# GpSimd subtracts one weight chunk of a tile instead of three in the first expert mixture

## The chip, the core and the metric

The kernel runs on one core of a Trainium2 chip. The metric is device time in microseconds (us) of one execution. The engines are named as the profile names them: PE is TensorE (matrix products), PEld its weight loads, DVE is VectorE, ACT is ScalarE, POOL is GpSimd, SP is SyncE, which issues most transfers.

## What is computed

An attention over 4 batches, 8 heads and 576 positions, whose weights far below the row's maximum are dropped, makes 2304 tokens of 512 numbers. They go through two mixtures of eight experts. An expert is two matrix products with a rectifier between them. The first mixture sends a token to its best expert; the second deals the tokens out so that each expert gets 288.

```python
# first mixture (cut)
e_idx = np.argmax(x @ w_gate, axis=1)
for e in range(E):                      # E = 8, D = 512, F = 1024
    mask = e_idx == e
    h = np.maximum(x[mask] @ w1[e], 0.0)
    ye = h @ w2[e]
    out[mask] = gate_w[mask, None] * eom[mask, e, None] * ye
```

## The kernel before

The first mixture, `moe1`, works on tiles of 128 tokens of one expert: 23 tiles (0 to 22), and two more that are only run if the routing needs them. `run` goes over the tiles, one turn of its loop for each. The order on each engine is that in which the code is written.

The weights of an expert come as eight chunks of 128x1024: chunks 0 to 3 are rows of `w1`, chunks 4 to 7 rows of `w2`. For a product of nearly float32 accuracy each chunk is split: `wh` is the chunk rounded (a cast on ScalarE, L609), `wl` is the chunk minus `wh` (L610 on GpSimd, L611 on VectorE). TensorE then makes three products for each pair of operands, high by high, high by low and low by high. Activations are split in the same way: `xh` and `xl` from the transposed tokens (L621), `hh` and `hl` from the transposed hidden layer (L649, L650). A chunk is split again for each tile that uses it.

`split(t,c)` splits chunk c for tile t and issues SyncE's conditional load of that chunk for the next expert. `splits(n)` calls it along a list: chunks 0 to 3 of tile t+2 come after chunks 4 to 7 of tile t. There are seven buffers each for `wh` and `wl`, so a cast waits until TensorE is done with the chunk seven places earlier.

A turn t does this, in the order of the code: `splits` issues chunks 4, 5 and 6 of tile t; `mm1` makes the first half of tile t+1's first product (L633 to L635); `ey` evicts the finished output y of tile t-1 from PSUM on VectorE (L667); `hT` transposes the hidden layer of tile t (Th, L647) and splits it into hh and hl; `splits` issues chunk 7 of tile t and chunk 0 of tile t+2; `mm1` makes the rest of tile t+1's first product; `yT` transposes y (Ty, L673); GpSimd gathers the tokens of tile t+3 (L615); `xT` transposes those of tile t+2 (Tx, L619) and splits them; in odd turns `logits2` transposes two tiles' router sums (Tl, L684); `splits` issues chunks 1, 2 and 3 of tile t+2; `mm2` makes tile t's second product (L660 to L662); in even turns `logits` makes the router sums. Th, Ty, Tx, Tl and those sums share three PSUM buffers (`psT`), handed out in turn, so a transpose waits until the reader of the one three places back is done. In turn 21 VectorE also finds a maximum between y and hl (`reach`, with a copy fmb of one row, L696).

Who subtracts is decided in `split`: GpSimd takes chunk 2 from tile 3 on, chunk 5 from tile 1 on and chunk 7 from tile 2 on; VectorE takes the rest.

Of the kernel before, what the change touches and what calls it, by code (L numbers as in the profile page):

```python
# [9 lines left out]
F32 = mybir.dt.float32  # L10
# [549 lines left out]
def moe1(tc, K, r, rts, xd, w1, w2, wg2, ys, LG2, reach_, ahead):  # L560
# [3 lines left out]
    nc=tc.nc; ident=K['ident']; N=NT1  # L564
    with ExitStack() as ctx:
# [7 lines left out]
        def rv(c,par): return raw[c][:,ds(par,1),:].rearrange("p a f -> p (a f)")  # L573
# [25 lines left out]
        def prefetch(t,c):  # L599
            q=regs[t]; nc.sync.dma_start(rvd(c,q['o']),src(q['n'],c),cond=q['c'],cond_hint=(t%3==0))  # L600
# [6 lines left out]
        def split(t,c):  # L607
            q=regs[t]; h,l=wtile()
            nc.scalar.copy(h,rv(c,q['a']))  # L609
            if t>(2 if c==2 else 0 if c==5 else 1 if c==7 else N): nc.gpsimd.tensor_sub(l,rv(c,q['p']),h.bitcast(F32))  # L610
            else: nc.vector.tensor_sub(l,rv(c,q['v']),h.bitcast(F32))  # L611
            prefetch(t,c); W[t,c]=(h,l)
        def gather(t):
# [97 lines left out]
        def splits(ahead):  # L711

            nonlocal pos
            while pos<min(used+ahead,ends[cur[0]]):
                t,c=order[pos]; pos+=1
                if c==0: regload(t)
                if t==0 and c<6: prefetch(t,c)
                else: split(t,c)
# [412 lines left out]
```

## Time and profile before

| what | value |
|---|---|
| median of 3 runs (lowest to highest) | 946.09 us (945.7 to 946.3) |
| profiled execution, its own time | 945.42 us |
| span of the profile | 943.6 us |
| busy over the span: PE, DVE, ACT, POOL | 94%, 77%, 67%, 41% |
| mean granted TensorE clock | 0.981 of full speed |
| first mixture, first and last VectorE subtraction | 341.3 to 644.3 us |

The busy shares are means over stages with different limits: attention, the first mixture, the routing of the second, the second mixture. The change touches the first mixture alone, so its stretch is what to read. A row of a timeline gives the start and the duration; rows of one kind that follow without a gap are merged, with their count (x3) and their whole duration; in brackets stands the idle time before, and what ended it.

### The profile page before, as it was taken

Reading aid. Unit: us, or ns where it says so; the run is one execution under the profiler, and the core shown is the slowest. Engines: PE = TensorE matmul, PEld = TensorE weight load, DVE = VectorE, ACT = ScalarE, POOL = GpSimd, SP = SyncE. Lnnn points to the kernel's source line nnn. Section 1 sums busy time; section 2 is a strip of 40 time slices with the busy share of each in tenths; the row PEclk is TensorE's granted clock in tenths of the full one; section 3 lists DMA queues with packets and bytes.
Section 4 is the critical chain, followed back from the end, with each engine's and each line's share of the span. In section 5 each row is a group of like instructions: output and inputs, shape, how many; then the busy total and the mean of one; then the engine's idle time right before and its main releaser. Section 6 shows DMA issues by size and latency. Waiting matters only on the chain. (4 is left out here: it accounts for less than half of the span.)

```text
span 943.6 us, 18044 instructions
## 1 busy us (share of the span) xinstructions
PE 886.3 (94%) x5939; PEld 733.2 (78%) x5939; DVE 725.2 (77%) x1191; ACT 635.6 (67%) x1070; POOL 384.7 (41%) x391
## 2 busy tenths in 40 slices
PE   7899999999999999899999999998779999999995
PEld 6677777777777667678787777786449999999994
DVE  5898988888888789798999998987755555555540
ACT  5787878878977677677787788774315555555541
POOL 4234323433431324577777776774030221122211
PEclk9999999999999999999999999999779999999998
DMA  7534444544331670155544655111535666666500
GB/s 190 149 88 124 122 118 115 130 128 115 104 83 53 221 259 25 44 163 185 170 154 148 211 168 182 43 36 46 180 117 180 194 192 186 179 193 203 162 26 25
DMA packets 69346, 127.64 MB, mean 135 GB/s; under 512 B 14912, under 2 KB 27200, under 8 KB 69248
## 3 DMA queue, kind: packets, MB, share of 16 engines
q1 hardware_dynamic: 64016, 109.91, 38.4%
q0 software_dynamic: 5232, 16.52, 5.6%
q8 instruction: 49, 0.80, 0.4%
q14 instruction: 49, 0.40, 0.1%
HBM read 159.70 MB, written 15.99 MB: 186 GB/s over the span
## 5 line engine op out<-in xcount | busy, mean ns | idle before, releaser
L611 DVE TENSOR_TENSOR wl<-raw,wh 128x1024 fp32r<-128x1024 f32 x115 | 218.1, 1916 | 28.4 <-ACT wh L609 28.1
L610 POOL TENSOR_TENSOR wl<-raw,wh 128x1024 fp32r<-128x1024 f32 x63 | 167.6, 2662 | 102.2 <-ACT wh L609 101.4
L609 ACT CAST wh<-raw 128x1024 fp32r x178 | 177.7, 1064 | 4.0 <-PE Y L662 3.3
L469 ACT ACTIVATE e<-S,nm 128x576 f32<-128x576 f32 x144 | 107.8, 749 | 55.0 <-DVE nm L464 54.6
L464 DVE TENSOR_REDUCE nm<-S 128x1 f32<-128x576 f32 x144 | 108.4, 757 | 21.8 <-PE S L388 10.6
L499 DVE SCALAR_TENSOR_TENSOR a<-S,th,e 128x576 f32<-128x576 f32 x144 | 114.4, 814 | 11.1 <-ACT e L469 4.8
L966 DVE TENSOR_TENSOR wl<-raw,wh 128x1024 fp32r<-128x1024 f32 x60 | 73.4, 1225 | 36.9 <-ACT wh L966 36.9
L1037 POOL DMA_INDIRECT out_dram<-o,it x24 | 22.4, 934 | 173.0 <-ACT o L1031 154.1
L397 PE MATMUL T<-ident,a 128*128 128x128 f32 x576 | 86.6, 273 | 0.0
L1008 PE MATMUL H<-xh,wh 128*128 128x288 f32 x256 | 77.8, 304 | 0.1
L1020 PE MATMUL Y<-hh,wh 128*128 128x288 f32 x256 | 77.5, 303 | 0.0
L318 POOL TENSOR_TENSOR ql<-f,QH 64x512 fp32r<-64x512 f32 x30 | 38.2, 1274 | 94.5 <-ACT f L317 76.4
L419 PE MATMUL O<-aT,v 128*64 128x288 f32 x512 | 75.8, 418 | 0.5 <-ACT xt L424 0.5
L1009 PE MATMUL H<-xl,wh 128*128 128x288 f32 x256 | 75.6, 295 | 0.2 <-DVE xl L1002 0.2
L633 PE MATMUL H<-wh,xh 128*128 128x512 f32 x184 | 75.1, 408 | 0.7 <-ACT xh L621 0.7
L1021 PE MATMUL Y<-hl,wh 128*128 128x288 f32 x256 | 75.5, 295 | 0.0
L1022 PE MATMUL Y<-hh,wl 128*128 128x288 f32 x256 | 75.5, 295 | 0.0
L402 ACT COPY aT<-T 128x512 f32<-128x512 f32 x128 | 75.2, 588 | 0.2 <-PE T L397 0.2
L660 PE MATMUL Y<-wh,hh 128*128 128x512 f32 x184 | 74.5, 405 | 0.9 <-ACT wh L609 0.9
L1010 PE MATMUL H<-xh,wl 128*128 128x288 f32 x256 | 75.3, 294 | 0.0
L662 PE MATMUL Y<-wh,hl 128*128 128x512 f32 x184 | 72.3, 393 | 0.0
L661 PE MATMUL Y<-wl,hh 128*128 128x512 f32 x184 | 72.3, 393 | 0.0
(344 smaller groups left out, 2130.4 us busy)
## 6 DMA issues: line engine op xcount, KB each, us to landing
raw<-in_moe_w_dram SPq DMA_DIRECT2D x256, 512.0 KB
ys<-y SPq DMA_DIRECT2D x23, 256.0 KB
q<-in_q_dram SPq DMA_DIRECT2D x16, 256.0 KB
k<-in_k_dram SPq DMA_DIRECT2D x16, 256.0 KB
v<-in_v_dram SPq DMA_DIRECT2D x16, 256.0 KB
QA<-QH SPq DMA_DIRECT2D x32, 128.0 KB
QB<-QH SPq DMA_DIRECT2D x32, 128.0 KB
xd<-xr SPq DMA_DIRECT2D x16, 256.0 KB
```

The lines of the kernel that those rows point to most:

```text
L397: for kb in (2*part,2*part+1): nc.tensor.transpose(TT[n][:,kb,:],a[:,o+kb*P:o+(kb+1)*P],ident)
L419: nc.tensor.matmul(O[hd*64:hd*64+64,:288],L['v'][:,hd,kb,:],aT[hd][:,kb,cs],start=kb==0,stop=False,skip_group_check=True)
L464: nc.vector.tensor_reduce(nm[:,i:i+1],S[i][:,:,:288],axis=AX.XY,op=ALU.max,negate=True)
L469: nc.scalar.activation(e[i],S[i][:,:,:288],AF.Exp,bias=nm[:,i:i+1])
L499: nc.vector.scalar_tensor_tensor(a[:,hd*576:hd*576+576].rearrange("p (a b) -> p a b",a=2),S[i][:,:,:288],th[:,i:i+1],e[i],op0=ALU.is_ge,op ...
L609: nc.scalar.copy(h,rv(c,q['a']))
L610: if t>(2 if c==2 else 0 if c==5 else 1 if c==7 else N): nc.gpsimd.tensor_sub(l,rv(c,q['p']),h.bitcast(F32))
L611: else: nc.vector.tensor_sub(l,rv(c,q['v']),h.bitcast(F32))
L1008: nc.tensor.matmul(H[:,:288],wh[:,fs],xh[:,kc],start=kc==0,stop=False)
L1009: nc.tensor.matmul(H[:,:288],wh[:,fs],xl[:,kc],start=False,stop=False)
L1020: nc.tensor.matmul(Y[:,:288],wh[:,ds_],h,start=f==0,stop=False)
L1021: nc.tensor.matmul(Y[:,:288],wh[:,ds_],l,start=False,stop=False)
```

## The change

One condition in `split`: which engine subtracts which chunk. GpSimd now takes chunk 6 from tile 2 on, and chunk 5 of tile 1. All the rest goes to VectorE. Casts, loads, products and buffers stay as they are.

```diff
             nc.scalar.copy(h,rv(c,q['a']))
-            if t>(2 if c==2 else 0 if c==5 else 1 if c==7 else N): nc.gpsimd.tensor_sub(l,rv(c,q['p']),h.bitcast(F32))
+            if t>0 and c==(5 if t==1 else 6): nc.gpsimd.tensor_sub(l,rv(c,q['p']),h.bitcast(F32))
             else: nc.vector.tensor_sub(l,rv(c,q['v']),h.bitcast(F32))
```

In the built program's order the chunks are told apart by their buffers: raw_4548 is chunk 0, raw_4549 chunk 1, and so on to raw_4555, chunk 7. A row ISA sets a register for the row after it, TENSOR_LOAD reads one.

VectorE at the start of turn 2, from chunk 0 of tile 3 to the eviction y of tile 1. Before:

```order
L611 TENSOR_TENSOR wl<-raw_4548,wh 128x1024
L611 ISA
L611 TENSOR_TENSOR wl<-raw_4549,wh 128x1024
L611 ISA
L611 TENSOR_TENSOR wl<-raw_4551,wh 128x1024
L611 ISA
L611 TENSOR_TENSOR wl<-raw_4552,wh 128x1024
L611 ISA
L611 TENSOR_TENSOR wl<-raw_4554,wh 128x1024
L667 TENSOR_SCALAR y<-Y,gs 128x512
```

And in the changed kernel, the same place on VectorE:

```order
L611 TENSOR_TENSOR wl<-raw_4548,wh 128x1024
L611 ISA
L611 TENSOR_TENSOR wl<-raw_4549,wh 128x1024
L611 ISA
L611 TENSOR_TENSOR wl<-raw_4550,wh 128x1024
L611 ISA
L611 TENSOR_TENSOR wl<-raw_4551,wh 128x1024
L611 ISA
L611 TENSOR_TENSOR wl<-raw_4552,wh 128x1024
L611 ISA
L611 TENSOR_TENSOR wl<-raw_4553,wh 128x1024
L667 TENSOR_SCALAR y<-Y,gs 128x512
```

Chunks 2 and 5 have come in ahead of y, and chunk 6 has left: six subtractions stand there instead of five, and the last one before y is that of chunk 5.

VectorE in an odd turn, from the last subtraction ahead of y to the first one behind xl (LG is the reading of the transposes Tl). Before:

```order
L611 TENSOR_TENSOR wl<-raw_4554,wh 128x1024
L667 TENSOR_SCALAR y<-Y,gs 128x512
L650 TENSOR_TENSOR hl<-Th,hh 128x512 x2
L605 TENSOR_LOAD tab
L605 ISA x2
L611 ISA
L611 TENSOR_TENSOR wl<-raw_4548,wh 128x1024
L621 TENSOR_TENSOR xl<-Tx,xh 128x512
L685 TENSOR_REDUCE LG_71<-Tl 128x16
L611 ISA
L611 TENSOR_TENSOR wl<-raw_4549,wh 128x1024
```

And in the changed kernel, the same stretch on VectorE:

```order
L611 TENSOR_TENSOR wl<-raw_4553,wh 128x1024
L667 TENSOR_SCALAR y<-Y,gs 128x512
L650 TENSOR_TENSOR hl<-Th,hh 128x512 x2
L611 ISA
L611 TENSOR_TENSOR wl<-raw_4555,wh 128x1024
L605 TENSOR_LOAD tab
L605 ISA x2
L611 ISA
L611 TENSOR_TENSOR wl<-raw_4548,wh 128x1024
L621 TENSOR_TENSOR xl<-Tx,xh 128x512
L685 TENSOR_REDUCE LG_71<-Tl 128x16
```

Chunk 7 has come in between hl and chunk 0 of the tile after next.

GpSimd, from one tile's last subtraction to the next tile's, in any turn from 3 on. Before:

```order
L610 TENSOR_TENSOR wl<-raw_4555,wh 128x1024
L605 TENSOR_LOAD tab
L605 ISA x2
L615 DMA x<-xd,ix_4728 128x512
L610 ISA
L610 TENSOR_TENSOR wl<-raw_4550,wh 128x1024
L610 ISA
L610 TENSOR_TENSOR wl<-raw_4553,wh 128x1024
L610 ISA
```

And in the changed kernel, on GpSimd:

```order
L610 TENSOR_TENSOR wl<-raw_4554,wh 128x1024
L605 TENSOR_LOAD tab
L605 ISA x2
L615 DMA x<-xd,ix_4728 128x512
L610 ISA
L610 TENSOR_TENSOR wl<-raw_4554,wh 128x1024
```

One subtraction and one gather are left in a turn, and the gather stands behind chunk 6 instead of chunk 7.

## Rows read from the trace of the kernel before

**Rows 1.** The page's costliest groups: the subtractions of both mixtures.

```profile
L611 DVE TENSOR_TENSOR wl<-raw,wh 128x1024 fp32r<-128x1024 f32 x115 | 218.1, 1916 | 28.4 <-ACT wh L609 28.1
L610 POOL TENSOR_TENSOR wl<-raw,wh 128x1024 fp32r<-128x1024 f32 x63 | 167.6, 2662 | 102.2 <-ACT wh L609 101.4
...
L966 DVE TENSOR_TENSOR wl<-raw,wh 128x1024 fp32r<-128x1024 f32 x60 | 73.4, 1225 | 36.9 <-ACT wh L966 36.9
```

**Rows 2.** Busy time by stretch: us, PE, PEld, DVE, ACT, POOL, PEclk, DMA.

```profile
380.00:385.00 5.00, 4.47 (x17) 3.66 (x18) 4.47 (x6) 3.60 (x5) 1.33 (x2) 0.66 0.38 108
480.00:520.00 40.00, 39.71 (x205) 32.32 (x204) 37.26 (x30) 32.32 (x43) 29.40 (x13) 1.00 0.43 146
```

**Rows 3.** TensorE's waits, 330 to 660 us: total us, times, longest.

```profile
PE Ty L673 <- DVE y L667: 5.4, 10, 3.5
```

**Rows 4.** Timeline of TensorE in an even turn: start, us, operation.

```profile
489.75 0.39 PE L634 MATMUL H<-wl,xh 128*128 128x512 f32 x1
489.98 0.40 PE L635 MATMUL H<-wh,xl 128*128 128x512 f32 x1
...
490.95 0.47 PE L660 MATMUL Y<-wh,hh 128*128 128x512 f32 x1
```

**Rows 5.** Timeline of TensorE in the odd turn after it.

```profile
503.42 0.39 PE L635 MATMUL H<-wh,xl 128*128 128x512 f32 x1
504.04 0.63 PE L673 MATMUL Ty<-ident,y 128*128 128x128 f32 x4 [0.23 <-DVE y L667]
...
505.14 0.44 PE L684 MATMUL Tl<-ident,ls 128*128 128x128 f32 x2
505.34 0.48 PE L660 MATMUL Y<-wh,hh 128*128 128x512 f32 x1
```

**Rows 6.** Timeline of TensorE in turn 2.

```profile
376.69 0.39 PE L635 MATMUL H<-wh,xl 128*128 128x512 f32 x1
380.53 0.63 PE L673 MATMUL Ty<-ident,y 128*128 128x128 f32 x4 [3.46 <-DVE y L667]
...
384.89 0.39 PE L662 MATMUL Y<-wh,hl 128*128 128x512 f32 x1
```

**Rows 7.** Timeline of TensorE in turn 21.

```profile
638.46 0.39 PE L635 MATMUL H<-wh,xl 128*128 128x512 f32 x1
...
642.00 0.48 PE L660 MATMUL Y<-wh,hh 128*128 128x512 f32 x1
```

**Rows 8.** Timeline of VectorE in the odd turn of rows 5.

```profile
498.67 1.23 DVE L611 TENSOR_TENSOR wl<-raw,wh 128x1024 fp32r<-128x1024 f32 x1 [0.66 <-ACT wh L609]
500.56 2.67 DVE L611 TENSOR_TENSOR wl<-raw,wh 128x1024 fp32r<-128x1024 f32 x1 [0.67 <-ACT wh L609]
503.15 0.74 DVE L667 TENSOR_SCALAR y<-Y,gs 128x512 f32<-128x512 f32 x1
503.81 1.27 DVE L650 TENSOR_TENSOR hl<-Th,hh 128x512 fp32r<-128x512 f32 x2
```

**Rows 9.** Timeline of GpSimd in the same turn.

```profile
499.66 2.49 POOL L610 TENSOR_TENSOR wl<-raw,wh 128x1024 fp32r<-128x1024 f32 x1 [2.73 <-ACT wh L609]
502.78 2.69 POOL L610 TENSOR_TENSOR wl<-raw,wh 128x1024 fp32r<-128x1024 f32 x1 [0.63 <-ACT wh L609]
```

**Rows 10.** Timeline of ScalarE in the same turn.

```profile
497.58 2.94 ACT L609 CAST wh<-raw 128x1024 fp32r x3
500.68 1.07 ACT L649 CAST hh<-Th 128x512 fp32r<-128x512 f32 x2
```

**Rows 11.** Timeline of VectorE ahead of y in turn 2.

```profile
367.40 12.32 DVE L611 TENSOR_TENSOR wl<-raw,wh 128x1024 fp32r<-128x1024 f32 x5
```

**Rows 12.** Timeline of ScalarE at the same place.

```profile
370.82 2.94 ACT L609 CAST wh<-raw 128x1024 fp32r x3
```

**Rows 13.** Timeline of VectorE in turn 21.

```profile
639.13 1.42 DVE L696 COPY fmb<-fm 1x128 f32<-1x128 f32 x1
```

**Rows 14.** Timeline of GpSimd in turn 21.

```profile
637.81 2.67 POOL L610 TENSOR_TENSOR wl<-raw,wh 128x1024 fp32r<-128x1024 f32 x1 [0.64 <-ACT wh L609]
```

## The prediction

> **What bounds the kernel now.** I read the page's costliest groups first. The change touches two lines of the same subtraction: VectorE does it 115 times at a mean of 1916 ns, GpSimd 63 times at 2662 ns, and the second mixture's copy of it, where GpSimd subtracts nothing, takes VectorE only 1225 ns for the same shape [rows 1]. So something in the first mixture makes VectorE's subtraction 0.69 us longer, 115 times.
>
> Then the busy time by stretch. In 40 us from the middle of the first mixture TensorE is busy for 39.71, VectorE for 37.26, ScalarE for 32.32, GpSimd for 29.40 [rows 2]. TensorE bounds the stage, so the change can give back only the time in which TensorE stands still and waits for VectorE. Those waits are few: ten times the transposes of a finished output tile (Ty, L673) wait for its eviction y (L667), 5.4 us in all, of which one wait is 3.5 [rows 3].
>
> A wait as the list shows it is less than what the turn loses, so I measure in TensorE's own order, from the start of the last matmul of L635 in a turn to the first one of L660. In an even turn, in which nothing waits, this is 489.98 to 490.95, 0.97 us; neighbouring matmuls start 0.23 us apart [rows 4]. An odd turn has two more transposes (Tl, 505.14 to 505.34, 0.20 us), so undisturbed it would take 1.17; it takes 503.42 to 505.34, 1.92 [rows 5]. So an odd turn loses 0.75 us: to y, then to the PSUM buffers that hl frees for Tx and Tl. Turns are 13.44 us apart (489.98 to 503.42).
>
> The long wait is in turn 2: 3.46 us for y. Behind it the transposes and nine matmuls, 376.69 to the start of 384.89, take 8.20 us [rows 6]. Undisturbed it would be 0.97 and then 8 steps of 0.23: 2.8. So this place loses 5.4 us, 3.46 of it the wait itself and most of the rest the clock: from 380 to 385 the granted clock is 0.66 of full speed [rows 2], a mixture of the 1.2 and 2.4 GHz levels after the engine had stood still.
>
> The third place is turn 21: from 638.46 to 642.00, 3.54 us against 1.17, a loss of 2.37 [rows 7].
>
> **Why VectorE is late there.** Lay VectorE's and GpSimd's rows of an odd turn side by side. The subtraction at 498.67 meets no GpSimd work and takes 1.23 us. The next, at 500.56, takes 2.67 and ends at 503.23 [rows 8]; GpSimd's subtraction runs from 499.66 to 502.15 [rows 9]. VectorE ends 1.08 us after GpSimd ends: it did nothing until then. In the other direction, GpSimd's next one starts at 502.78, while VectorE's subtraction runs to 503.23, and takes 2.69, ending 2.24 after that. The two subtractions exclude each other. But y (0.74) and both hl (1.27 for two) run at 503.15 and 503.81, inside that GpSimd row, at full speed: they read PSUM. So three GpSimd subtractions a tile hold up VectorE in SBUF work, except for what falls on y and hl.
>
> **The change, part by part.** From turn 3 on GpSimd loses chunks 2, 5 and 7 and gets 6: 63 subtractions become 22 (21 of chunk 6, and chunk 5 of tile 1 as before), and VectorE's 115 become 156.
>
> VectorE's load. Seven subtractions of 1.23, y 0.74, two hl 1.27 and xl, about as long as one hl (0.64): 11.3 us in a turn of 13.44. Now it is 37.26/40 of 13.44, 12.5. The two added subtractions cost 2.5 and the blocked time that goes is larger.
>
> Odd turns (3, 5, ... 19, nine of them). ScalarE's casts of chunks 4, 5, 6 run from 497.58 to 500.52, about 0.98 apart, and hh is done at 501.75 [rows 10]; these stay. VectorE: chunk 4 498.67 to 499.90, chunk 5 to 501.1, y to 501.85, both hl to 503.1. TensorE can ask for y at 503.65 (0.23 after its last L635), for the buffers of Tx and Tl at about 504.0 and 504.35. All come earlier by 1.2 us or more, so the 0.75 goes whole. GpSimd's chunk 6 has its cast at 500.52, must wait for VectorE's chunk 5 until 501.1, and takes 2.4: 503.5. Chunk 6 is read 12 matmuls into the second product, 504.6 + 12 x 0.23 = 507.4: hidden, and without cover up to 3.9 us of delay would cost nothing. Chunk 7, now behind hl on VectorE, waits for that port until 503.5 and ends at 504.7; it is read at 504.6 + 18 x 0.23 = 508.7. xl and the next chunk 0 stand behind it; ScalarE's part of xl comes after 505, as now. The even turns lose nothing now and have the same margins. Nine times 0.75 is 6.75 us.
>
> Turn 2. VectorE has five subtractions from 367.40 on that take 12.32 us, to 379.7, and then y [rows 11]. It will have six (chunks 0 to 3 of tile 3, then 4 and 5 of tile 2), with no GpSimd work beside them. Four end at 367.40 + 4 x 1.22 = 372.3; the casts of 4, 5, 6 end by 373.76 [rows 12], so 4 and 5 end at 374.7, y at 375.5, hl at 376.7. TensorE wants y at 376.92. The wait goes and with it the slow clock: 5.4 us. From both sides: nothing if another wait ends last there, 5.4 at most.
>
> Turn 21. A copy fmb of one row, between y and hl, takes 1.42 us and ends at 640.55 [rows 13], 0.07 after GpSimd's chunk 7 ends (637.81 + 2.67 = 640.48) [rows 14]. That subtraction moves to VectorE, behind hl. Chunk 6 is left ahead of fmb; placed as in an odd turn, where it ends 0.15 before Ty is wanted, it ends at about 638.5, so fmb at 638.6 and hl at 639.9, against 639.4 at which Tl wants it. Some 0.5 us stays: 2.37 - 0.5 = 1.9. The bounds are 1.0 (fmb held its whole 1.4 again) and 2.37.
>
> Other queues. GpSimd's gather stood behind chunk 7 and stands behind chunk 6: earlier. SyncE's conditional loads wait for each subtraction in order; those of 2, 5 and 7 are released sooner, that of 6 at 503.5 instead of 503.23. The stages behind the first mixture start from its last tile and move with it.
>
> Sum: 6.75 + 5.4 + 1.9 = 14.05 us. The profiled execution took 945.42 us (span 943.6), so 931.4; the median of the runs shown is 0.67 higher, 946.09, so **932.0 us**, 1.5% less.
>
> **A rule against it.** The row of 500.56 shows a float32 subtraction that takes 1.4 us longer than the one at 498.67 and ends 1.08 us after GpSimd's [rows 8, 9]. The Trainium skill, Advanced Engine Details and Errata, VectorE Performance Modes, ties the blocking of GpSimd and VectorE to VectorE's two-port modes, for which it names conditions; no row says whether this subtraction is in one. [...]
>
> **Rivals.** (1) The odd turns hand their wait on: ScalarE, 32.32 of 40 busy, or a PSUM buffer ends last instead of VectorE. For it: ScalarE's work does not shrink. Against: hh was done at 501.75, 1.9 us before Ty. Then only turns 2 and 21 pay: 945.42 - 7.3 + 0.67 = 938.8. Chance 0.12.
> (2) Turn 2 keeps its wait, because a cast or gather was about to end as late: 945.42 - 8.65 + 0.67 = 937.4. Chance 0.07.
> (3) Slower: VectorE is not given back what GpSimd took. Its subtractions stay at the present length for another reason, and two more of 1.23 make 12.5 + 2.46 = 15.0 us of work in a turn of 13.44, 1.5 over in each of 20 turns: 946.09 + 31 = 977. It decides from a net addition of 0.92 us a turn, the present idle time. The rows of 1225 ns and 1.23 speak against it. Chance 0.04.
> (4) No change that can be told: the waits move elsewhere in all three places. 946, chance 0.03.
> My forecast has the remaining 0.74.
>
> **How the numbers follow.** A measurement of this kernel can tell about 0.2%, 1.9 us. The forecast alone, with the bounds of turn 21 and a few tenths in the nine odd turns, is 930 to 934. The range must also take in rivals 1 and 2: 929.5 to 939. Faster 0.93 (forecast and rivals 1, 2), same 0.03, slower 0.04.
>
> **What would show it.** VectorE's subtraction in the mixture should fall from 1916 ns to under 1400, its busy share there below 90%; the ten waits of Ty for y should be gone, the clock between turns 2 and 3 full, and the three distances 0.97, 1.17 and about 1.7 us. It is wrong if Tx or Ty wait for a ScalarE line, if L661 or L634 wait for wl, or if VectorE's subtractions keep 1.9 us.

## The result and the profile after

The changed kernel takes 931.34 us (median of 4 runs, 930.74 to 931.51), the kernel before 946.19 beside it: a ratio of 0.9841, 95% interval 0.9825 to 0.9856. The forecast was 932.0, with 929.5 to 939.0 as its range. The profiled execution took 930.74 us, its span is 928.6 against 943.6.

The page's groups of the subtractions, after (answering to [rows 1]):

```profile
L611 DVE TENSOR_TENSOR wl<-raw,wh 128x1024 fp32r<-128x1024 f32 x156 | 187.9, 1256 | 23.7 <-ACT wh L609 21.2
...
L610 POOL TENSOR_TENSOR wl<-raw,wh 128x1024 fp32r<-128x1024 f32 x22 | 63.4, 2882 | 197.4 <-ACT wh L609 91.1
```

VectorE makes 41 subtractions more and is busy with them for 30 us less: their mean fell from 1916 to 1256 ns, next to the 1225 of the second mixture. The busy time by stretch (us, PE, PEld, DVE, ACT, POOL, PEclk, DMA; answering to [rows 2]):

```profile
370.00:380.00 10.00, 10.00 (x54) 8.40 (x53) 9.72 (x11) 9.92 (x15) 4.49 (x2) 1.00 0.17 54
380.00:385.00 5.00, 5.00 (x28) 3.58 (x27) 3.28 (x4) 3.01 (x5) 0.00 (x0) 1.00 0.01 2
480.00:520.00 40.00, 40.00 (x214) 32.43 (x213) 32.91 (x35) 33.21 (x45) 11.32 (x6) 1.00 0.43 141
```

In the middle of the mixture TensorE is busy for 40.00 of 40 us instead of 39.71, VectorE for 32.91 instead of 37.26, GpSimd for 11.32 instead of 29.40. Where the clock had fallen to 0.66 after turn 2 it is now 1.00 throughout.

TensorE's waits from 330 to 660 us (total, times, longest; answering to [rows 3]); the ten waits of Ty for y are gone, and a new one stands there, for A:

```profile
PE cn L836 <- DVE G L832: 4.4, 2, 3.2
PE Ty L673 <- DVE A L698: 1.1, 1, 1.1
```

(The row of cn belongs to the routing of the second mixture, which has moved into this window.) The timeline of TensorE: an even turn, an odd turn, turn 2 and turn 21, from the last matmul of L635 to the first of L660 (answering to [rows 4 to 7]):

```profile
480.35 0.40 PE L635 MATMUL H<-wh,xl 128*128 128x512 f32 x1
...
481.31 0.46 PE L660 MATMUL Y<-wh,hh 128*128 128x512 f32 x1
...
493.77 0.40 PE L635 MATMUL H<-wh,xl 128*128 128x512 f32 x1
494.00 0.60 PE L673 MATMUL Ty<-ident,y 128*128 128x128 f32 x4
494.36 0.54 PE L619 MATMUL Tx<-identr,x 128*128 128x128 f32 x4
494.74 0.41 PE L684 MATMUL Tl<-ident,ls 128*128 128x128 f32 x2
494.90 0.48 PE L660 MATMUL Y<-wh,hh 128*128 128x512 f32 x1
...
375.46 0.39 PE L635 MATMUL H<-wh,xl 128*128 128x512 f32 x1
375.69 0.60 PE L673 MATMUL Ty<-ident,y 128*128 128x128 f32 x4
...
376.42 0.46 PE L660 MATMUL Y<-wh,hh 128*128 128x512 f32 x1
...
624.89 0.40 PE L635 MATMUL H<-wh,xl 128*128 128x512 f32 x1
...
626.27 0.48 PE L660 MATMUL Y<-wh,hh 128*128 128x512 f32 x1
```

The distances are 0.96, 1.13, 0.96 and 1.38 us, where they were 0.97, 1.92, 4.75 and 3.54. Nothing in brackets stands at Ty: it no longer waits for y. (The 4.75 of turn 2 is 376.69 to 381.44; the prediction's 8.20 takes in eight matmuls more.) The timeline of VectorE in the odd turn and ahead of y in turn 2, and behind it that of GpSimd in the odd turn (answering to [rows 8, 9, 11]):

```profile
489.02 2.36 DVE L611 TENSOR_TENSOR wl<-raw,wh 128x1024 fp32r<-128x1024 f32 x2 [1.71 <-ACT wh L609]
491.29 0.74 DVE L667 TENSOR_SCALAR y<-Y,gs 128x512 f32<-128x512 f32 x1
491.95 1.28 DVE L650 TENSOR_TENSOR hl<-Th,hh 128x512 fp32r<-128x512 f32 x2
493.15 2.71 DVE L611 TENSOR_TENSOR wl<-raw,wh 128x1024 fp32r<-128x1024 f32 x2
...
366.57 6.89 DVE L611 TENSOR_TENSOR wl<-raw,wh 128x1024 fp32r<-128x1024 f32 x6
373.38 0.74 DVE L667 TENSOR_SCALAR y<-Y,gs 128x512 f32<-128x512 f32 x1
```

```profile
491.02 2.63 POOL L610 TENSOR_TENSOR wl<-raw,wh 128x1024 fp32r<-128x1024 f32 x1 [10.87 <-PE Th L647]
```

GpSimd's one subtraction lies over y and hl, which run at full speed, as the prediction laid it. y starts 2.7 us and ends 2.0 us before Ty is wanted (491.29 and 492.03 against 494.00); in turn 2 six subtractions take 6.89 us where five took 12.32.

**The sum of the two profiles.** From the last L635 of turn 2 to that of turn 21 the kernel before took 638.46 - 376.69 = 261.77 us, the changed one 624.89 - 375.46 = 249.43: 12.34 less. Turn 21 gives 2.16. From the first L660 of turn 21 to the end it is 302.3 against 301.6 us: 0.7 given back. The remaining 1.23 us lie ahead of turn 2's last L635, in two parts.

The first 0.93 us lie ahead of turn 1's last L635 (361.58 before, 360.65 after), and so ahead of every instruction that the change moves; in the second profile of the changed kernel, below, that place is at 361.81, as late as before. This part is the scatter of one execution. The other 0.30 us lie between those two places (15.11 us before, 14.81 in both profiles of the changed kernel) and belong to the change. In the kernel before, VectorE's chunks 0 and 1 of tile 3 take 4.55 us, beside GpSimd's chunk 2, and end at 371.95; TensorE's first product with the low part of chunk 1 (L634) starts 0.48 us after the matmul ahead of it, where neighbours start 0.23 apart:

```profile
367.40 4.55 DVE L611 TENSOR_TENSOR wl<-raw,wh 128x1024 fp32r<-128x1024 f32 x2
...
371.53 0.40 PE L633 MATMUL H<-wh,xh 128*128 128x512 f32 x1
372.01 0.50 PE L634 MATMUL H<-wl,xh 128*128 128x512 f32 x1
```

In the changed kernel four subtractions take 4.62 us there. So 14.1 us of the 15.0 between the two profiles are the change.

### The profile page after: what moved, and what is told of

Read it like the earlier page. It is cut to its first block, busy times and chain, and to the rows that moved or that the text cites. A ratio compares the mean times of both kernels' runs of the same rounds, so it can differ in the third digit from the quotient of the medians.

```text
span 928.6 us, 18051 instructions
## 1 busy us (share of the span) xinstructions
PE 879.3 (95%) x5939; PEld 732.7 (79%) x5939; DVE 698.1 (75%) x1232; ACT 632.6 (68%) x1070; POOL 272.8 (29%) x350
## 5 line engine op out<-in xcount | busy, mean ns | idle before, releaser
L611 DVE TENSOR_TENSOR wl<-raw,wh 128x1024 fp32r<-128x1024 f32 x156 | 187.9, 1256 | 23.7 <-ACT wh L609 21.2
L609 ACT CAST wh<-raw 128x1024 fp32r x178 | 175.8, 1068 | 0.6 <-DMA raw<-in_moe_w_dram 0.4
L610 POOL TENSOR_TENSOR wl<-raw,wh 128x1024 fp32r<-128x1024 f32 x22 | 63.4, 2882 | 197.4 <-ACT wh L609 91.1
L966 DVE TENSOR_TENSOR wl<-raw,wh 128x1024 fp32r<-128x1024 f32 x60 | 73.4, 1225 | 36.8 <-ACT wh L966 36.8
L660 PE MATMUL Y<-wh,hh 128*128 128x512 f32 x184 | 73.9, 401 | 0.9 <-DVE y L667 0.9
L635 PE MATMUL H<-wh,xl 128*128 128x512 f32 x184 | 72.2, 392 | 0.0
L634 PE MATMUL H<-wl,xh 128*128 128x512 f32 x184 | 71.7, 390 | 0.0
```

## The experiments

The question after the result was not whether the waits went, but what took them away: fewer subtractions on GpSimd, or the place of the one that is left. The theory is the prediction's: a subtraction on GpSimd and one on VectorE exclude each other, so what counts is what VectorE still has to do ahead of y when GpSimd runs. Rivals: only the number counts; or VectorE's order and ScalarE's casts set its pace, whatever GpSimd does. Each ratio below is to the kernel before, run on the same chip.

**One subtraction, in the wrong place** (e1_chunk5): chunk 5 from tile 1 on, and no other.

```diff
-            if t>0 and c==(5 if t==1 else 6): nc.gpsimd.tensor_sub(...)
+            if t>0 and c==5: nc.gpsimd.tensor_sub(...)
```

> One GpSimd subtraction a tile as in the changed kernel, but chunk 5 instead of chunk 6, so the number is kept and the place is undone. If the two subtractions exclude each other: VectorE's chunk 6 is held behind GpSimd's chunk 5, y starts in an odd turn at the old place, and the distance from the last L635 to the first L660 stays 1.9 us instead of 1.13 in the nine odd turns (6.9 us); turn 2 goes from 0.96 to about 1.8; turn 21 to about 2.3 from 1.38. Together 8 to 9 us more than the changed kernel: 939 to 940. If only the number of GpSimd subtractions counts: 931 to 932, with odd turns of 1.13.

Measured: 940.27 us, ratio 0.9933 (0.9908 to 0.9958). VectorE's timeline in an odd turn, GpSimd's, and TensorE's:

```profile
493.24 1.23 DVE L611 TENSOR_TENSOR wl<-raw,wh 128x1024 fp32r<-128x1024 f32 x1 [1.70 <-ACT wh L609]
495.14 2.66 DVE L611 TENSOR_TENSOR wl<-raw,wh 128x1024 fp32r<-128x1024 f32 x1 [0.68 <-ACT wh L609]
497.72 0.74 DVE L667 TENSOR_SCALAR y<-Y,gs 128x512 f32<-128x512 f32 x1
```

```profile
494.29 2.42 POOL L610 TENSOR_TENSOR wl<-raw,wh 128x1024 fp32r<-128x1024 f32 x1 [9.61 <-ACT wh L609]
```

```profile
498.00 0.39 PE L635 MATMUL H<-wh,xl 128*128 128x512 f32 x1
498.61 0.63 PE L673 MATMUL Ty<-ident,y 128*128 128x128 f32 x4 [0.23 <-DVE y L667]
...
499.90 0.48 PE L660 MATMUL Y<-wh,hh 128*128 128x512 f32 x1
```

The picture of [rows 8, 9] is back with a third of GpSimd's work: a subtraction of 2.66 us ahead of y that ends 1.09 after GpSimd's, a wait of 0.23, a distance of 1.90. Turn 2 has 1.82 and turn 21 2.33, as expected. In the even turns GpSimd is the one that waits: its subtraction takes 5.07 us (from 478.50), and VectorE's three beside it take 3.48. The number alone gives 6 of the 15 us, in turn 2 and turn 21; the odd turns between keep their 1.9.

**Three subtractions, in the right place** (e3_three_placed): chunks 2, 6 and 7 instead of 2, 5 and 7.

```diff
-            if t>0 and c==(5 if t==1 else 6): nc.gpsimd.tensor_sub(...)
+            if c==5 if t==1 else t>1 and c in (6,7) or t>2 and c==2: nc.gpsimd.tensor_sub(...)
```

> Three GpSimd subtractions a tile as in the kernel before, but chunks 2, 6 and 7 instead of 2, 5 and 7, so the number is undone and the place is kept. If it counts what VectorE does ahead of y: y stands behind chunk 5, which nothing holds, and is in time; odd turns 1.13 to 1.3, turn 2 near 0.97, turn 21 up to the old 3.5, VectorE's mean subtraction 1.7 us or more: 931 to 936. If the number of GpSimd subtractions counts: nearly all of the old time, 943 to 946, with odd turns of 1.9.

Measured: 940.79 us, ratio 0.9951 (0.9932 to 0.997): outside both expectations. The odd turns are indeed free, 500.74 to 501.87, 1.13 us, in TensorE's timeline; now the even turns wait, 1.87 us, where they had 0.97:

```profile
486.42 0.39 PE L635 MATMUL H<-wh,xl 128*128 128x512 f32 x1
487.33 0.66 PE L673 MATMUL Ty<-ident,y 128*128 128x128 f32 x4 [0.52 <-DVE y L667]
...
488.29 0.47 PE L660 MATMUL Y<-wh,hh 128*128 128x512 f32 x1
...
500.74 0.40 PE L635 MATMUL H<-wh,xl 128*128 128x512 f32 x1
...
501.87 0.48 PE L660 MATMUL Y<-wh,hh 128*128 128x512 f32 x1
```

VectorE's timeline ahead of that even turn, and GpSimd's, say why:

```profile
478.99 7.62 DVE L611 TENSOR_TENSOR wl<-raw,wh 128x1024 fp32r<-128x1024 f32 x3 [0.19 <-ACT wh L609]
486.53 0.74 DVE L667 TENSOR_SCALAR y<-Y,gs 128x512 f32<-128x512 f32 x1
```

```profile
478.09 2.98 POOL L610 TENSOR_TENSOR wl<-raw,wh 128x1024 fp32r<-128x1024 f32 x1 [0.31 <-ACT wh L609]
481.87 2.52 POOL L610 TENSOR_TENSOR wl<-raw,wh 128x1024 fp32r<-128x1024 f32 x1 [0.81 <-ACT wh L609]
```

Chunk 6 has its cast earlier in an even turn, so GpSimd starts it at 481.87 while VectorE still has chunks 4 and 5 ahead of y, and chunk 2 had held VectorE just before: three subtractions take 7.62 us instead of 3.5. So the place is right only as long as VectorE has no backlog, and the number decides that. Either half of the change gives about 6 us by the medians, the two together 15. The turns between 2 and 21 gain from neither half alone: from the last L635 of turn 3 to that of turn 21 the kernel before takes 243.0 us (395.44 to 638.46), e1_chunk5 243.2 (389.88 to 633.12), this version 244.2 (392.17 to 636.40), and the changed kernel 236.0 (388.90 to 624.89). What each half gains lies in turn 2, with the clock behind it, and in turn 21.

**GpSimd's work without VectorE's relief** (e4_dummies): the changed kernel, and two more subtractions a tile on GpSimd, from tile 3 on, of a spare tile from itself. They add work whose result nobody reads.

```diff
+        zz=rp.tile([P,1024],BF16,name="zz"); nc.gpsimd.memset(zz,0.0)
...
+            if t>2 and c in (2,7): nc.gpsimd.tensor_sub(zz,zz,zz)
```

> The changed kernel, and GpSimd makes two more subtractions a tile of a spare 128x1024 bfloat16 tile from itself, which nobody waits for. VectorE's work and its order are unchanged. If GpSimd's subtractions hold VectorE's while they run: VectorE has 11.3 us of its own and up to 2 x 2.3 us held, more than a turn of 13.1 holds, its mean subtraction rises from 1256 to 1700 ns or more, and each of 20 turns gets up to 2.5 us longer: 940 to 980. If VectorE's long subtractions came from its order or its casts: no change, 931 to 932, mean 1256.

Measured: 998.78 us, ratio 1.0567 (1.0545 to 1.0589), above the upper end. The page's groups:

```profile
L612 DVE TENSOR_TENSOR wl<-raw,wh 128x1024 fp32r<-128x1024 f32 x156 | 261.7, 1727 | 29.0 <-ACT wh L610 29.0
...
L613 POOL TENSOR_TENSOR zz<-zz 128x1024 bf16<-128x1024 bf16 x40 | 96.8, 2421 | 0.4
```

and TensorE's waits from 330 to 660 us (lines below the dummy are two higher here):

```profile
PE Ty L675 <- DVE y L669: 25.6, 8, 3.2
PE Tx L621 <- DMA x<-xd,ri: 8.0, 1, 8.0
```

VectorE's own list is untouched, yet its 156 subtractions went from 1256 to 1727 ns, 74 us in all for 40 GpSimd subtractions, 1.8 us each. The order or the casts can't have done that: this rival falls. Not all of the 67 us are from this: turn 2's last L635 comes 11.5 us later than in the changed kernel (386.96 against 375.46), ahead of every dummy but the first. 8.0 of that is the wait for the first gather, which starts at 337.01 instead of 330.66 in the kernel before; the profile puts its wait down to a weight load, and why the spare tile brings that about isn't shown. From turn 2's L635 to turn 21's it is 301.3 us against 249.4, 52 for 19 turns, with the clock falling again after waits of 3.2 us.

**No subtraction on GpSimd** (e2_none): VectorE takes all from tile 2 on.

```diff
-            if t>0 and c==(5 if t==1 else 6): nc.gpsimd.tensor_sub(...)
+            if t==1 and c==5: nc.gpsimd.tensor_sub(...)
```

> VectorE makes every subtraction from tile 2 on; only chunk 5 of tile 1 stays on GpSimd. If GpSimd's subtraction is only a hindrance: VectorE has 8 x 1.22 + 2.65 = 12.4 us of work in a turn of 13.1 and still keeps ahead, the wait of 1.1 us in turn 22 goes (chunk 7 is no longer held), turn 21 falls from 1.38 towards 1.2: 929.5 to 931. If VectorE needs GpSimd's help, because it waits between its subtractions for casts and for hh and can't use all its idle time: y or hl come too late in the turns, 0.2 us or more in each of 20 turns, 936 or more.

Measured: 930.2 us, ratio 0.9844 (0.9822 to 0.9866). All turns have 0.96 and 1.13 as in the changed kernel, turn 21 1.27, and Ty no longer waits for A. In the stretch from 480 to 520 VectorE is busy for 34.51 us and TensorE for all 40:

```profile
480.00:520.00 40.00, 40.00 (x213) 32.41 (x213) 34.51 (x37) 33.21 (x46) 3.47 (x3) 1.00 0.41 142
```

So the well placed subtraction that is left gives TensorE nothing; it only does no harm in 19 turns out of 21.

Whether a little is to be had there, the second set tells, all on one chip, with the **changed kernel again** (e5_changed_again) beside it:

> The changed kernel once more, beside the next three on the same chip: 931.0 to 931.7, so that they can be compared with it.

Measured: 932.38 us (931.94 to 932.81), ratio 0.9854 (0.9839 to 0.9869): a little above the expectation. Its profile has the same distances (1.40 in turn 21), and turn 2's last L635, too, is as late as in the kernel before:

```profile
376.62 0.40 PE L635 MATMUL H<-wh,xl 128*128 128x512 f32 x1
```

**The last tile to VectorE** (e6_not_last_tile):

```diff
-            if t>0 and c==(5 if t==1 else 6): nc.gpsimd.tensor_sub(...)
+            if 0<t<22 and c==(5 if t==1 else 6): nc.gpsimd.tensor_sub(...)
```

> The changed kernel, but GpSimd subtracts nothing for the last tile of the run, 22. If the wait of 1.1 us of Ty for A in turn 22 comes from VectorE's chunk 7 being held behind GpSimd's chunk 6 (it took 3.25 us there): that wait goes, the time from the last L635 of turn 21 to the end falls from 303.7 to 302.6 us, and the median by 0.8 to 1.1, to 930.2 to 930.6. If the wait has another cause: no change.

Measured: 929.86 us (929.03 to 930.72), ratio 0.9825 (0.9811 to 0.9838). VectorE's timeline in turn 22 in the changed kernel (its first profile), TensorE's, and VectorE's in this one:

```profile
628.95 4.54 DVE L611 TENSOR_TENSOR wl<-raw,wh 128x1024 fp32r<-128x1024 f32 x2
633.41 0.74 DVE L667 TENSOR_SCALAR y<-Y,gs 128x512 f32<-128x512 f32 x1
```

```profile
634.27 0.66 PE L673 MATMUL Ty<-ident,y 128*128 128x128 f32 x4 [1.11 <-DVE A L698]
```

```profile
629.85 3.47 DVE L611 TENSOR_TENSOR wl<-raw,wh 128x1024 fp32r<-128x1024 f32 x3
633.25 0.73 DVE L667 TENSOR_SCALAR y<-Y,gs 128x512 f32<-128x512 f32 x1
```

Three subtractions take 3.47 us where two took 4.54, and the wait for A is gone: its cause is shown. From turn 21's L635 to the end the profiles give 303.16 against 303.91 us, 0.75 less than in the changed kernel's second one; the medians differ by 2.5. The profile of this version is that of its slowest execution (930.72 us, the others 929.03 to 930.61), so the two profiles understate the difference; what makes up the rest they don't show. This is the lowest median of the study, by less than the runs scatter.

**No GpSimd subtraction, again** (e7_none_again), the same edit as e2_none:

> The kernel without GpSimd's subtractions from tile 2 on, again. If GpSimd's one well placed subtraction gives TensorE nothing and only costs in turns 21 and 22: 1.1 to 1.3 us less than the changed kernel on the same chip, 930.0 to 930.5. If its 930.20 was chance: the same as the changed kernel within 0.4 us.

Measured: 930.59 us (929.21 to 932.42), ratio 0.9829 (0.9815 to 0.9842): 1.8 less than the changed kernel beside it, with one of its five runs (932.42) as slow as that kernel's and the others at 930.62 or below; and not to be told from the version above.

**None at all** (e8_none_at_all): chunk 5 of tile 1 goes to VectorE too.

```diff
-            if t>0 and c==(5 if t==1 else 6): nc.gpsimd.tensor_sub(...)
-            else: nc.vector.tensor_sub(l,rv(c,q['v']),h.bitcast(F32))
+            nc.vector.tensor_sub(l,rv(c,q['v']),h.bitcast(F32))
```

> VectorE makes every subtraction, chunk 5 of tile 1 too. There VectorE has other work between its subtractions (hl, the gate's reading, y) that is read from PSUM or waits for TensorE; one more of 1.22 us ahead of them can delay hl of tile 1 by up to 0.3 us. Same as the kernel without GpSimd's subtractions from tile 2 on, within 0.5 us: 929.7 to 930.7.

Measured: 932.84 us (932.33 to 933.21), ratio 0.9856 (0.9841 to 0.9871): 2 us more than expected. TensorE's timeline in turn 1, here and in e7_none_again (one line lower here), and the busy time from 365 to 370 us, here and there:

```profile
365.35 0.47 PE L659 MATMUL Y<-wh,hh 128*128 128x512 f32 x1 [1.53 <-DVE y L666]
```

```profile
364.14 0.48 PE L660 MATMUL Y<-wh,hh 128*128 128x512 f32 x1 [0.86 <-ACT wh L609]
```

```profile
365.00:370.00 5.00, 4.65 (x14) 3.68 (x14) 5.00 (x7) 4.76 (x6) 0.10 (x1) 0.66 0.42 110
...
365.00:370.00 5.00, 5.00 (x25) 4.10 (x24) 5.00 (x6) 4.28 (x6) 2.51 (x2) 1.00 0.69 209
```

In turn 1 VectorE is the late engine here: the one PSUM buffer for Y must be evicted as y before TensorE goes on, and 1.2 us more ahead of y make the wait 1.53 instead of 0.86. (In e7_none_again y ends at 364.00, and the profile puts the end of the wait down to a cast that ended about as late.) Behind the wait the granted clock is 0.66, where e7_none_again has 1.00, and that costs more than the wait: from this L659 to turn 2's last L635 it takes 13.81 us (365.35 to 379.16) instead of 12.21 (364.14 to 376.35), 1.6 more, against 0.67 more of waiting. Here GpSimd's help is worth its price.

## Why the prediction was right, step by step

**The exclusion of the two subtractions** was read from one pair of rows. e4_dummies shows it on VectorE's unchanged list (1256 to 1727 ns). The section of the Trainium skill that the prediction names, Advanced Engine Details and Errata, VectorE Performance Modes, speaks of two-port modes alone, and its table gives a tensor_tensor none; but the same page, under GPSIMD Details, names VectorE instructions with two SBUF inputs as well, and this subtraction has two. The runs agree with the latter: VectorE's subtraction is held in [rows 8, 9] and in e1_chunk5, 2.67 and 2.66 us instead of 1.23.

**Odd turns**: 0.75 forecast, 0.76 to 0.79 measured in each of nine (1.89 to 1.92 before, 1.12 or 1.13 after). y was forecast to end 1.8 us ahead of its need and ends 2.0 ahead. **Turn 2**: 5.4 forecast; the distance falls by 3.79 and the clock stays full; the two steps together were to give 12.15, and 12.34 is measured between turns 2 and 21. **Turn 21**: 1.9 forecast, 2.16 measured. The copy fmb is still held, as was said, and for as long as before (1.46 us from 623.36, against 0.21 in e2_none). But y is earlier, so that fmb ends 0.07 before the last L635 instead of 2.09 behind it. The distance is 1.38 against the 1.27 of e2_none: the hold costs 0.11, and not the 1.4 at which the lower bound of this step put a copy held that long. **Rivals 1 to 4** did not come: ScalarE is busier (33.21 of 40 us) and nothing waits for it there, and VectorE has less to do than before (32.91 against 37.26).

**What was missed** is turn 22. The text gave the remaining GpSimd subtraction a price in turn 21 alone; in the last tile VectorE's chunk 7, now ahead of y and A, is held behind it, and 0.7 us are given back. e6_not_last_tile shows the cause. Missed on the other side were the 0.30 us ahead of turn 2's last L635. The sum was 14.05 us, and the profiles show 14.1 from the change and 0.9 more that is scatter. That the two agree so closely is in part luck: 0.7 too much stands against 0.2, 0.3 and 0.3 too little.

Open: why the medians of the changed kernel and e6_not_last_tile differ by more than their profiles do.

## What to carry to other kernels

An engine that takes work off a busy one can cost it more than it takes: compare the mean of the same instruction with and without the helper beside it (1916 and 1225 ns here) before counting instructions. What helper work is left belongs over operations of the busy engine that it doesn't disturb, here those that read PSUM, and the place holds only while the busy engine has no backlog. A wait that makes the granted clock fall is worth more than its length, so look at those first.

## What was not expected of the hardware

A bfloat16 subtraction of 128x1024 on GpSimd took 1901 to 2891 ns (mean 2421). The shortest float32 one in the kernel before took 2382, so half the bytes saved a fifth of the time, and the bfloat16 one held VectorE like it. And a wait of 1.53 us ahead of L659 was followed by a granted clock of 0.66 over the next 5 us (a mean between the two levels, 1.2 and 2.4 GHz), while one of 0.86 us at the same place was followed by full speed.
